# A fused chunk-selecting attention and gated feed-forward kernel: nine wide filler products as 36 narrow ones, and block 4's transposes ahead of two loads

## The chip, the cores and the metric

The kernel runs on one core of a Trainium2 chip. The metric is the device time of one execution in microseconds (us). A comparison takes the median of several runs. The profiled execution is one further run, whose instructions and transfers were all recorded; its times count from the first instruction.

## What is computed

Attention over 4 batches of 8 heads, 768 tokens and 64 elements a head, followed by a feed-forward layer. Each query picks, of the chunks of 32 keys up to its own, the six with the highest upper bound of the score, and attends to their keys alone:

```python
k_min, k_max = k_chunks.min(axis=3), k_chunks.max(axis=3)
ub = np.maximum(q * k_min, q * k_max).sum(-1)        # per query and chunk
ub = np.where(causal, ub, -1e9)
top_chunks = np.argsort(ub, axis=-1)[..., -6:]
scores = np.where(sel & (key <= query), scale * q @ k.T, -1e9)
x = softmax(scores) @ v                              # 3072 tokens x 512
xn = x / sqrt(mean(x * x) + 1e-6) * rms_g
g = xn @ w_gate                                      # 512 x 1536
out = (g * sigmoid(g) * (xn @ w_val)) @ w_out        # 1536 x 512
```

## The kernel before, in words

**Blocks.** The work is cut into twelve blocks of 256 queries of one batch, numbered in the order `ORDER` of line 340; block 4 is batch 0, queries 256 to 511, which the trace's steps call `(0, 1)`. A block goes through two stages. Attention (`job` and `pick`, lines 486 to 859): load q and k (`load_qk`, line 431), turn them on VectorE (line 636), reduce k's chunks (line 651), upper bounds on TensorE (lines 522 and 540), the choice on VectorE (lines 565 to 593), masked scores on TensorE (lines 760 and 771), exponentials on ScalarE (line 810), products with v (line 836), normalised x (line 855). Feed-forward (`norm` and `ffn`, lines 862 to 1032): x is scaled by its root mean square, transposed into `xsT`, multiplied with the gate and value weights (line 960), and the gated result with the output weights (line 1008).

**The order is written out by hand.** Each step of the program is an operation `plan.op` with a number. The list `STEPS` (line 47) says in which order the operations are issued, over all engines; each engine executes its own in that order. An entry x of zero or more is operation x // 8 on engine x % 8 (0 TensorE, 1 ScalarE, 2 VectorE, 3 GpSimd, 4 SyncE). `SLOTS` (line 156) gives, in the order of `STEPS`, the buffer that each operation takes. Semaphores follow from what each instruction reads and writes.

**Fillers.** A negative entry puts products between the steps of TensorE that nobody reads, into a PSUM buffer that is free at that place; they keep TensorE at work while it would wait. In `run`, line 236, the entry is decoded: `n, slot = divmod(-x, 16)`, then n // 2 products into buffer `slot`, wide if n is odd. Line 1075 issues them: the identity as weights, and as the moving side the identity once (narrow, 128 columns) or four times over (wide, 512 columns). Each product is two instructions of TensorE, a weight load and the product. Fillers wait for nothing but their PSUM buffer. Before the first upper bounds stand 75 narrow ones; 39 wide ones follow in the first 33 us.

**Block 4's way to `xsT`.** From block 4 on, the transposition of x is done by DMA (`norm`, lines 885 to 900). For each half of 128 tokens: `scale4s` on VectorE (line 890) multiplies x by its factor and the weights of the norm and writes a buffer `xs`; `across4s` on SyncE (line 896) issues a DMA that writes the transposed half into `xsT`. The gate products of block 4 (line 960) read both halves. SyncE also issues all loads of q and k (line 376, loads of 64 KB) and all stores (line 1030), one after the other; a step that waits holds up everything behind it on this queue. The steps of SyncE around the place are, in the order before: store of block 2's second half, two loads of q for block 8 (`load q1210`, `load q1220`: batch 1, third block, part, group), `across40`, `across41`, `load q1201`, then four copies of q between partitions (line 706).

Of the kernel before, what the change touches and what calls it, by code (L numbers as in the profile page):

```python
# [33 lines left out]
class Plan:  # L34
# [13 lines left out]
        131, 228, 233, 123, 155, 3, 99, 249, 244, 27, 257, 276, 83, 34, 203, 281, 67, 268, 107, 291,  # L48
        75, 115, 412, 425, 299, 433, 420, 538, 139, 466, 380, 396, 473, 482, 490, 404, 545, 42, 498,
        388, 522, 506, 515, 179, 594, 529, 611, 315, -2080, -320, 616, 562, 601, 672, 554, 626, 571,  # L50
        681, 50, 578, 457, 786, 587, 634, 323, -82, -82, 792, 642, 689, 57, 848, 650, 802, 699, 810,
        9, 818, 857, 307, 658, 865, 665, 826, 875, 834, 1098, -176, 704, 841, 443, -80, 736, 912,
        713, 746, 922, 754, 721, 1107, 930, 1185, 1042, -82, -114, 880, 451, 1114, 1049, 1058, 19,
        731, 889, 1066, 331, 897, 1130, 961, 1075, -338, -114, 1248, 1170, 760, 1257, 1082, 1091,
        907, 1660, 1177, 195, 971, -83, 936, 1628, -80, 1192, 1644, 1362, 977, 1138, 1684, 1265,
        1676, 1202, 1147, 1210, -112, 984, 1668, 770, 1154, 1163, 778, 1123, 1636, 946, -49, 1368,
        954, 1652, 1218, 1001, 1275, 994, 1424, 1433, 1226, -51, 1312, 1378, 8384, 1011, 1234, 1441,
        1322, 1242, 1386, 8344, 1330, 147, 1451, 1017, 1394, 1402, 339, 1280, 1410, 8369, 1418,
        1024, 1289, 1488, 347, 8336, 1498, 1297, 1034, 355, 8401, 1506, 1456, 8353, 8480, 1307,
        8410, 1537, 363, 8362, 1336, 8497, 8488, 1547, 1346, 1473, 1762, 8528, 1465, 8506, 1851,  # L60
# [30 lines left out]
        3323, 4940, 9377, 4980, 3339, 3256, 3353, 4972, 3842, 3280, 4900, 9584, 4459, 3290, 3361,  # L91
        4932, 3266, 3850, 9531, 9632, 3274, 9601, 3298, 3857, 3368, 9610, 5548, 3392, 3378, 9649,
        4956, 9627, 9640, 3386, 3402, 4964, 3417, 3410, 3864, 5580, 9658, 4275, 3425, 5644, 9680,
        5002, 3873, 9356, 4363, 5106, 4948, 3889, 3435, 5564, 5066, 9665, 9388, 3458, 3904, 4465,
        5628, 3442, 9675, 5612, 9712, 3913, 5018, 3883, 3452, 5026, 3899, 3921, 5090, 3468, 5042,
        3976, 5082, 4472, 5059, 3985, 5604, 5122, 5035, 4411, 4001, 9688, 4482, 3995, 9720, 9697,
        5139, 4016, 4490, 4498, 5049, 4011, 5148, 3928, 9729, 6308, 3952, 4025, 3938, 6356, 5098,
        9792, 3962, 4506, 5172, 4033, 9840, 3970, 5156, 3946, 9809, 4514, 5164, 4040, 9865, 9800,
        9818, 5620, 4521, 6332, 4050, 5714, 9832, 5572, 5114, 5588, 4592, 9849, 5179, 5652, 4058,
# [67 lines left out]
        0, 0, 1, 0, 2, 11, 3, 1, 0, 3, 0, 1, 1, 0, 2, 1, 1, 1, 1, 0, 1, 0, 0, 2, 3, 4, 1, 0, 6, 1,  # L167
        0, 0, 1, 0, 1, 2, 0, 1, 2, 2, 1, 0, 0, 2, 1, 0, 0, 0, 1, 3, 0, 1, 0, 1, 2, 0, 2, 3, 3, 0, 7,
        12, 2, 1, 0, 1, 0, 0, 0, 3, 0, 2, 3, 1, 0, 2, 8, 1, 2, 2, 3, 2, 0, 1, 2, 2, 1, 9, 3, 0, 1,
        0, 2, 0, 1, 0, 13, 0, 0, 0, 1, 0, 1, 10, 2, 1, 4, 0, 1, 1, 0, 1, 3, 1, 2, 0, 0, 1, 1, 0, 0,  # L170
        3, 1, 0, 0, 3, 3, 1, 0, 2, 0, 2, 4, 5, 0, 0, 3, 2, 1, 0, 0, 0, 0, 2, 1, 0, 2, 0, 0, 11, 3,
        14, 2, 1, 15, 1, 1, 2, 2, 0, 1, 1, 0, 0, 1, 3, 1, 2, 2, 0, 0, 3, 1, 2, 0, 0, 0, 1, 0, 2, 0,
        4, 1, 1, 2, 1, 0, 1, 3, 1, 2, 4, 1, 0, 0, 1, 2, 1, 0, 1, 1, 3, 1, 2, 1, 3, 0, 0, 16, 0, 2,
        2, 5, 0, 1, 0, 1, 0, 3, 0, 0, 1, 1, 1, 2, 0, 12, 0, 2, 1, 0, 1, 1, 3, 9, 0, 2, 1, 1, 2, 0,
        1, 5, 2, 3, 0, 0, 1, 1, 1, 0, 2, 1, 0, 6, 1, 3, 2, 2, 0, 2, 2, 1, 0, 0, 1, 0, 0, 1, 7, 8, 0,
        3, 2, 12, 9, 1, 0, 0, 1, 1, 1, 0, 2, 3, 0, 2, 1, 3, 0, 2, 1, 0, 0, 1, 0, 3, 2, 0, 2, 2, 0,
        3, 0, 2, 0, 0, 0, 1, 1, 0, 1, 2, 0, 0, 0, 3, 0, 4, 0, 13, 1, 1, 1, 0, 1, 0, 3, 2, 0, 1, 0,
        0, 2, 0, 2, 10, 0, 2, 3, 1, 1, 1, 1, 1, 1, 0, 0, 2, 2, 1, 0, 0, 0, 1, 1, 5, 1, 3, 1, 0, 2,
        0, 2, 0, 11, 1, 0, 0, 0, 0, 3, 2, 0, 3, 3, 3, 12, 1, 0, 1, 1, 1, 5, 0, 2, 4, 1, 0, 0, 2, 3,
        1, 0, 0, 0, 1, 0, 1, 2, 2, 2, 0, 3, 1, 1, 1, 0, 0, 2, 1, 0, 0, 2, 0, 3, 0, 0, 2, 0, 1, 1, 3,  # L180
        4, 1, 1, 0, 1, 2, 2, 2, 1, 1, 3, 0, 0, 0, 0, 1, 0, 2, 1, 2, 3, 0, 3, 2, 1, 2, 8, 0, 2, 3, 2,
        0, 6, 1, 0, 1, 2, 1, 8, 1, 9, 0, 0, 2, 3, 0, 0, 1, 1, 0, 0, 1, 0, 2, 1, 1, 0, 2, 0, 0, 0, 3,
        1, 2, 1, 0, 2, 2, 2, 0, 0, 1, 0, 7, 1, 3, 3, 1, 0, 2, 2, 2, 0, 0, 1, 1, 3, 1, 2, 9, 1, 0, 2,
        1, 0, 3, 0, 2, 2, 1, 3, 1, 1, 0, 5, 2, 0, 1, 1, 0, 3, 10, 2, 2, 0, 2, 1, 2, 3, 2, 1, 0, 0,
        11, 0, 3, 1, 3, 1, 0, 2, 0, 1, 1, 0, 0, 2, 12, 1, 1, 1, 0, 0, 0, 2, 1, 0, 2, 2, 2, 1, 2, 3,
        1, 0, 4, 6, 1, 0, 1, 3, 2, 1, 1, 0, 2, 5, 1, 1, 0, 0, 1, 0, 0, 2, 0, 1, 0, 3, 1, 2, 8, 0, 4,
        3, 1, 0, 1, 3, 2, 2, 2, 2, 0, 0, 1, 1, 3, 0, 2, 2, 0, 2, 3, 1, 9, 3, 0, 0, 2, 2, 0, 1, 2, 3,
        1, 5, 2, 0, 1, 1, 2, 0, 0, 2, 1, 0, 3, 2, 10, 0, 1, 11, 0, 1, 2, 2, 3, 1, 0, 0, 2, 0, 2, 7,
        3, 0, 2, 0, 2, 0, 3, 1, 0, 4, 3, 0, 6, 1, 0, 1, 3, 0, 12, 2, 0, 0, 1,
# [917 lines left out]
```

## Time and profile before

| | |
|---|---|
| time, median of 3 runs | 291.84 us (291.59 to 293.34) |
| the profiled execution's own time | 291.08 us |
| its span, first to last instruction | 289.3 us |
| its mean granted TensorE clock | 1.000 |
| ScalarE busy | 206.6 us (71%) |
| GpSimd busy | 168.4 us (58%) |
| VectorE busy | 216.3 us (75%) |
| data moved by DMA | 31.94 MB, mean 110 GB/s |

In the profile PE is TensorE's products, PEld its weight loads, DVE is VectorE, ACT ScalarE, POOL GpSimd, SP SyncE; an engine's name with a q is its instruction queue. A row of a timeline gives the start, the length, the engine, the line of the kernel, the operation, what it writes and reads, how many instructions were merged, and in brackets the idle time before and what ended it. A row of windows gives the stretch, its length, and for the engine the busy time and the number of instructions; then the granted clock, the DMA share and the rate. A row of a DMA queue gives packets, MB, and the share of 16 DMA engines that the packets took.

### The profile page before, as it was taken

The page shows a single profiled execution, that of the slowest core. Times are in us where ns is not written, and L with a number is a line of the kernel's source. Part 1 is how long each engine was busy: PE and PEld are TensorE (multiplying, and loading weights), DVE is VectorE, ACT ScalarE, POOL GpSimd, SP SyncE. Part 2 cuts the span into 40 slices and gives each one's busy share as a digit, 9 for nine tenths or more (in the row PEclk, how much of TensorE's full clock was granted, in tenths as well). Part 3 has the DMA queues.
Part 4 walks back from the last instruction along what each step waited for, and adds up shares of the span by engine and source line. Part 5 has one row for each costly group of instructions (what it writes and reads, how often), then busy time and mean ns, then how long its engine had stood idle before and what let it go on. Part 6 is the DMA issues. An engine that isn't in the chain of part 4 may idle for free.

```text
span 289.3 us, 11429 instructions
## 1 busy us (share of the span) xinstructions
PE 278.8 (96%) x4706; PEld 214.8 (74%) x4734; DVE 216.3 (75%) x626; ACT 206.6 (71%) x355; POOL 168.4 (58%) x268
## 2 busy tenths in 40 slices
PE   7998999999999997999999999999999999999995
PEld 7646997758877856888776786788678967588763
DVE  3889788798998998699989999987574724274332
ACT  2976787778988987867966695877679767564421
POOL 6797789979987874567693485527225206112420
PEclk9999999999999999999999999999999999999999
DMA  8999999988499495468699506902012200303013
GB/s 189 195 193 243 207 202 141 149 149 131 108 172 157 117 189 94 108 97 160 99 180 145 148 22 102 128 5 75 2 36 78 22 2 3 111 18 58 0 49 134
DMA packets 86388, 31.94 MB, mean 110 GB/s; under 512 B 74816, under 2 KB 81728, under 8 KB 86336
## 3 DMA queue, kind: packets, MB, share of 16 engines
q1 hardware_dynamic: 55616, 22.56, 34.0%
q0 software_dynamic: 29712, 7.87, 27.4%
q10 hardware_dynamic: 1008, 0.79, 1.3%
q8 instruction: 37, 0.61, 0.9%
q14 instruction: 15, 0.12, 0.1%
HBM read 28.58 MB, written 6.29 MB: 121 GB/s over the span
## 4 chain that ended last, share of the span: by engine, by line
PE 90%; DMA 4%; ACT 2%; SPq 1%; issue 1%; DVE 1%; ACTq 0%
PE F L960 45%; PE F L1008 19%; PE S L760 8%; PE F L836 7%; PE F L1075 3%; PE S L771 3%; PE F L522 3%; PE F L540 1%; DMA xsT<-xs 1%; SPq L376 1%; DMA kraw<-in_k_dram 1%; DMA qraw<-in_q_dram 1%; ACT kb L643 1%; PE F L916 1%; DVE kx L651 1%
## 5 line engine op out<-in xcount | busy, mean ns | idle before, releaser
L810 ACT ACTIVATE pt<-S 128x1024 bf16<-128x1024 f32 (+3 forms) x104 | 85.5, 858 | 29.8 <-PE S L771 25.9
L982 POOL TENSOR_TENSOR hh<-tg,vs 128x512 bf16<-128x512 bf16 x48 | 55.6, 1167 | 44.4 <-DVE tg L971 27.5
L960 PE MATMUL F<-xsT,wg 128*128 128x256 bf16 (+1 forms) x640 | 72.2, 262 | 1.5 <-DMA xsT<-xs 1.5
L960 PE MATMUL F<-xsT,wv 128*128 128x256 bf16 (+1 forms) x640 | 71.6, 262 | 0.1
L971 DVE SCALAR_TENSOR_TENSOR tg<-th,F 128x512 bf16<-128x512 bf16 x72 | 48.4, 679 | 25.9 <-ACT th L967 20.5
L1008 PE MATMUL F<-wo,hh 128*128 128x512 bf16 (+1 forms) x272 | 65.5, 370 | 1.8 <-issue 0.6
L960 PEld LDWEIGHTS <-wg 128*128 128x128 bf16 x640 | 56.0, 98 | 10.3 <-issue 2.0
L960 PEld LDWEIGHTS <-wv 128*128 128x128 bf16 x640 | 56.2, 98 | 7.8 <-issue 0.2
L967 ACT ACTIVATE th<-F 128x512 bf16<-128x512 f32 x72 | 42.6, 599 | 13.8 <-PE F L960 12.6
L780 POOL TENSOR_SCALAR_AFFINE_SELECT pt<-pt 128x512 bf16<-128x512 bf16 x48 | 31.9, 670 | 26.5 <-ACT pt L810 26.4
L1008 PEld LDWEIGHTS <-hh 128*128 128x128 bf16 x300 | 27.6, 98 | 25.2 <-issue 0.4
L979 ACT ACTIVATE vs<-F 128x512 bf16<-128x512 f32 x48 | 28.5, 599 | 9.6 <-PE F L960 6.4
L760 PE MATMUL S<-qb,kb 32*128 32x256 bf16 (+1 forms) x800 | 32.9, 253 | 1.2 <-issue 1.0
L651 DVE TENSOR_REDUCE kx<-kT 128x16 f32<-128x512 f32 x48 | 31.1, 670 | 0.2
L836 PEld LDWEIGHTS <-pt 128*128 128x128 bf16 x672 | 25.4, 98 | 3.8 <-issue 0.2
L836 PE MATMUL F<-VX,pt 128*128 128x65 bf16 x672 | 27.4, 194 | 0.2
L760 PEld LDWEIGHTS <-kb 32*128 32x128 bf16 x800 | 13.9, 92 | 14.2 <-issue 12.8
L975 DVE TENSOR_TENSOR hh<-tg,F 128x512 bf16<-128x512 bf16 x24 | 16.1, 682 | 10.4 <-PE F L960 10.1
L376 POOL DMA_DIRECT2D VX<-in_v_dram x24 | 22.8, 952 | 0.0
L771 PE MATMUL S<-mtd,chunkrow 32*128 32x128 bf16 (+2 forms) x384 | 20.4, 203 | 0.0
L855 DVE TENSOR_TENSOR xnat<-F,rden 128x256 bf16<-128x256 f32 x48 | 19.5, 415 | 0.7
L771 PE MATMUL S<-mto,chunkrow 32*128 32x128 bf16 (+2 forms) x384 | 19.9, 203 | 0.0
(73 smaller groups left out, 339.1 us busy)
## 6 DMA issues: line engine op xcount, KB each, us to landing
out_dram<-osb SPq DMA_DIRECT2D x23, 256.0 KB, 3.3
kraw<-in_k_dram SPq DMA_DIRECT2D x72, 64.0 KB, 3.2
qraw<-in_q_dram SPq DMA_DIRECT2D x72, 64.0 KB, 3.2
VX<-in_v_dram POOLq DMA_DIRECT2D x24, 128.0 KB, 4.9
QX<-qT SPq DMA_DIRECT2D x32, 64.0 KB, 2.8
wv<-in_moe_w_val_dram POOLq DMA_DIRECT2D x3, 512.0 KB, 9.7
wg<-in_moe_w_gate_dram POOLq DMA_DIRECT2D x3, 512.0 KB, 8.6
wo<-in_moe_w_out_dram POOLq DMA_DIRECT2D x3, 512.0 KB, 11.5
```

The lines of the kernel that those rows point to most:

```text
L651: plan.op(f"ext{n}{J}", "DVE", 0.585, 0.67, lambda n=n, op=op: VE.tensor_reduce(out=at(kx)[:, g, n], in_=at(kT).rearrange("p h (j c x) -> ...
L760: TE.matmul(s[a // 2][:, a % 2, c0:c0 + q1 - q0], kbt[r, t, ks], qbt[r, t, q0:q1], start=(t == 0), stop=(t == 1 and not mask), skip_group_ ...
L771: TE.matmul(o, chunkrow[r, BLK * kg + P * e:BLK * kg + P * (e + 1)], mv, start=False, stop=(d == 1), skip_group_check=True)
L780: GE.affine_select(out=d, in_=d, compare_op=ALU.is_ge, fill=0.0, base=0, pattern=[[0, 4], [1, P]], channel_multiplier=-1)
L810: lambda pt=pt, hs=hs, c0=c0, c1=c1, x=sc[hp]: SE.activation(out=at(pt)[:, hs, c0:c1], in_=at(x)[:, :, c0:c1], func=ACT.Exp, scale=SCALE), ...
L836: TE.matmul(o[:, a, :], p_[:, a, off:off + P], vt[:, e, 4 * g + a, :], start=(kb_ == 0 and a == 0), stop=(kb_ == nkb - 1 and a == 3), skip ...
L960: TE.matmul(at(p_)[:, n * W:(n + 1) * W], w[:, g, ht * P:(ht + 1) * P], at(xT)[:, g, x0:x0 + W], start=(g == 0), stop=(g == NP - 1), skip_ ...
L967: plan.op(f"tanh{U}.{hp}", "ACT", 0.48, 0.6, lambda th=th, gp=gp: SE.activation(out=at(th), in_=at(gp), func=ACT.Tanh, scale=0.5), pri - 0 ...
L971: VE.scalar_tensor_tensor(out=at(tg), in0=at(th), scalar=1.0, in1=at(gp), op0=ALU.add, op1=ALU.mult), pri - 30, reads=[th, gp], writes=[tg ...
L979: plan.op(f"vcopy{U}.{hp}", "ACT", 0.48, 0.6, lambda vs=vs, vp=vp: SE.activation(out=at(vs), in_=at(vp), func=ACT.Copy), pri + 0.1, reads= ...
L982: plan.op(f"hh{U}.{hp}", "POOL", 1.11, 1.16, lambda tg=tg, vs=vs, hh=hh: GE.tensor_tensor(out=at(hh), in0=at(tg), in1=at(vs), op=ALU.mult) ...
L1008: TE.matmul(at(op)[:, cs], at(key)[:, o:o + P], wo[:, ht, cs], start=(ht == 0), stop=(ht == NHT - 1), skip_group_check=True)
```

## The change

Two things are edited, both in the lists. First, three negative entries near the start of `STEPS`. Before, `-82, -82` stand for two and two wide products into buffer 2, ahead of the upper bounds of block 0's second group of heads; now `-514` stands for 16 narrow ones into the same buffer. Before, `-176` stands for five wide products into buffer 0, ahead of the first masked scores; now `-640` stands for 20 narrow ones. The columns that are computed stay the same, 9 x 512 = 36 x 128. TensorE has 27 more products and 27 more weight loads, so 54 more instructions, ahead of all that follows. Counted in blocks of 256 instructions of TensorE, each later limit falls on an instruction that came 54 earlier in the program before.

```diff
-        681, 50, 578, 457, 786, 587, 634, 323, -82, -82, 792, 642, 689, 57, 848, 650, 802, 699, 810,
-        9, 818, 857, 307, 658, 865, 665, 826, 875, 834, 1098, -176, 704, 841, 443, -80, 736, 912,
+        681, 50, 578, 457, 786, 587, 634, 323, -514, 792, 642, 689, 57, 848, 650, 802, 699, 810, 9,
+        818, 857, 307, 658, 865, 665, 826, 875, 834, 1098, -640, 704, 841, 443, -80, 736, 912, 713,
```

Second, the steps around block 4's transposes. 3458 and 3442 are `scale41` and `scale40` on VectorE, which change places; 3452 and 3468 are `across40` and `across41` on SyncE; 5628 and 5612 are `load q1210` and `load q1220`, which go behind them one by one (5604 is `load q1201`):

```diff
-        5002, 3873, 9356, 4363, 5106, 4948, 3889, 3435, 5564, 5066, 9665, 9388, 3458, 3904, 4465,
-        5628, 3442, 9675, 5612, 9712, 3913, 5018, 3883, 3452, 5026, 3899, 3921, 5090, 3468, 5042,
-        3976, 5082, 4472, 5059, 3985, 5604, 5122, 5035, 4411, 4001, 9688, 4482, 3995, 9720, 9697,
+        5002, 3873, 9356, 4363, 5106, 4948, 3889, 3435, 5564, 5066, 9665, 9388, 3442, 3904, 4465,
+        3458, 9675, 9712, 3452, 3913, 5018, 3883, 5026, 3899, 3921, 5628, 5090, 3468, 5042, 3976,
+        5082, 4472, 5059, 5612, 3985, 5122, 5035, 5604, 4411, 4001, 9688, 4482, 3995, 9720, 9697,
```

| | SyncE's order | VectorE's order |
|---|---|---|
| before | store 2.1, load q1210, load q1220, across40, across41, load q1201 | scale41, scale40 |
| after | store 2.1, across40, load q1210, across41, load q1220, load q1201 | scale40, scale41 |

The orders of TensorE, ScalarE and GpSimd stay as they were. `SLOTS` changes in five lines: the two halves of blocks 4, 6, 8 and 10 change their `xs` buffers with each other, and those of blocks 7 and 10 their buffers of x (`xnat`).

20 rows, old and new, of tables (SLOTS, STEPS) are left out of this document.

## The prediction

> **What bounds the kernel now.** I read the page first, then the waits of TensorE, then TensorE's timeline around its two longest waits, and last the DMA view and the other queues at those two places.
>
> ```profile
> span 289.3 us, 11429 instructions
> ...
> PE 278.8 (96%) x4706; PEld 214.8 (74%) x4734; DVE 216.3 (75%) x626; ACT 206.6 (71%) x355; POOL 168.4 (58%) x268
> ...
> q8 instruction: 37, 0.61, 0.9%
> ...
> PE 90%; DMA 4%; ACT 2%; SPq 1%; issue 1%; DVE 1%; ACTq 0%
> ```
>
> The first line is the span. The profiled execution took 291.08 us, so 1.8 us lie around the span; it is 0.8 us below the median of the three runs, 291.84. TensorE (PE) is busy for 96% of the span, and the chain that ended last lies on it for 90%. So a time that TensorE gains or loses is a time of the whole kernel, unless a later wait takes it up. The q8 line is a queue that carries nothing but instructions: 37 packets, 0.61 MB, 16.5 KB each. TensorE's recorded instructions, 4706 products (PE) and 4734 weight loads (PEld), divided by 37 give 255: one packet is one block of 256 instructions of TensorE.
>
> ```profile
> PE F L960 <- DMA xsT<-xs: 1.5, 1, 1.5
> PE S L760 <- issue: 1.0, 1, 1.0
> PE F L1008 <- issue: 0.6, 4, 0.2
> ```
>
> These rows give who waited for whom, the total in us, how often, and the longest. After its start TensorE stands still twice for over 1 us. The first wait is for the transposed x of a block (xsT), the second "for issue", which means that no semaphore explains it. The third row is four pieces of at most 0.2 us. So 2.5 us are all that could be won in the middle of the run, and both parts of the change point at one of these places.
>
> ```profile
> 27.69 0.10 PEld L760 LDWEIGHTS <-kb 32*128 32x128 bf16 x4
> 28.96 0.10 PEld L760 LDWEIGHTS <-kb 32*128 32x128 bf16 x4 [1.17 <-issue]
> ```
>
> In the timeline of the weight loads the second wait is seen from close by. It falls inside the scores of block 1: four loads at 27.69, and the next four of the same line only at 28.96, 1.17 us idle. Nothing that TensorE would wait for lies between two such groups, so I take it for a block of instructions that was not there yet. That can be tested with positions. The windows below count weight loads from the start (the number behind the x); each product has one load, so twice the count is the position in the program.
>
> ```profile
> 0.00:9.06 9.06, 6.78 (x93) 1.00 0.98 187
> 0.00:15.44 15.44, 10.23 (x221) 1.00 1.19 191
> 0.00:22.90 22.90, 14.23 (x349) 1.00 1.30 192
> 0.00:28.50 28.50, 18.56 (x477) 1.00 1.27 205
> 0.00:35.38 35.38, 24.84 (x606) 1.00 1.27 205
> ```
>
> The stall comes after load 477 (row to 28.50). One block earlier, 128 loads, is load 349, issued at 22.90; another 128 earlier, less one for two semaphore instructions between, is load 222, issued at 15.44; then load 94 at about 9.06; and one block behind the stall is 605 at 35.38. Now the packets of q8, in four windows of the DMA view of 0.2 us each: 12.6 to 12.8, 26.3 to 26.5, 32.8 to 33.0, 38.6 to 38.8. Each row is one packet that begins there; its share times 16 engines times 0.2 us is its length.
>
> ```profile
> q8 instruction: 1, 0.02, 37.8%
> q8 instruction: 1, 0.02, 36.1%
> q8 instruction: 1, 0.02, 32.1%
> q8 instruction: 1, 0.02, 27.9%
> ```
>
> The lengths are 1.21, 1.16, 1.03 and 0.89 us. So TensorE enters a block at 9.06 and a packet begins at 12.7; it enters one at 22.90 and a packet begins at 26.4, ends at 27.56, and TensorE goes on at 28.96, 1.4 us after the packet's end; it enters one at 28.96, and a packet begins at 32.9. I read this as: **on entering a block TensorE asks for the next one, and here it can use that block 6.06 us later** (22.90 to 28.96). A block that takes longer than that costs nothing, a shorter one stalls. From 9.06 to 15.44 it was 6.38 us, from 28.96 to 35.38 it was 6.42: both just long enough. The limits in this stage are all close to a stall, and 54 instructions decide it.
>
> **The change, part 1: nine wide products become 36 narrow ones.** The durations first.
>
> ```profile
> 9.84 1.04 PE L1075 MATMUL F<-ident 128*128 128x512 bf16 x4
> 10.91 0.44 PE L540 MATMUL F<-qT,BO 64*64 64x32 f32 x16
> 11.84 1.25 PE L1075 MATMUL F<-ident 128*128 128x512 bf16 x5
> 13.02 0.29 PE L760 MATMUL S<-qb,kb 32*128 32x128 bf16 x8
> ```
> ```profile
> 2.00:5.50 3.50, 3.43 (x34) 1.00 0.98 279
> 7.00:8.50 1.50, 1.48 (x27) 1.00 1.46 187
> ```
>
> Four wide products lie between 9.84 and the second upper bounds at 10.91, five between 11.84 and the scores at 13.02: 1.07 and 1.18 us, waits at their ends included. Of narrow ones, 34 loads fall into 3.5 us early on (103 ns each) and 27 into 1.5 us later (56 ns each). At 56 ns the new 16 take 0.90 us and the new 20 take 1.12 us, 0.2 us less than the wide ones; at the early rate they take 1.65 and 2.06 us, 1.5 us more. I take the later rate, which lies nearest in time, and count nothing, since what follows hides either: TensorE comes to a block that is not there for 1.9 us. If that cover is gone, -0.2 to +1.5 us counts.
>
> The cost is the place of the limits. 27 more products are 54 more instructions, all of them in by load 163 of today. So from there on a limit that stood at load n now stands where load n-27 stands today. The limit of load 222 moves to load 195, that of 349 to 322, of 477 to 450, of 605 to 578. When are these issued today?
>
> ```profile
> 0.00:13.36 13.36, 9.20 (x195) 1.00 1.17 191
> 0.00:22.14 22.14, 13.73 (x323) 1.00 1.29 192
> 0.00:27.04 27.04, 17.92 (x451) 1.00 1.28 206
> 0.00:33.87 33.87, 23.33 (x578) 1.00 1.27 205
> ```
>
> At 13.36, 22.14, 27.04 and 33.87. Now the sum, limit by limit.
> - Load 195, 13.36: the block is asked for at 9.06 as before, since nothing before 9.84 changes. Its packet ends at 12.7 + 1.2 = 13.9, and 1.4 us later, at 15.3, it can be used. **TensorE stands from 13.36 to 15.3, 1.9 us.** Bounds: 0.5 us if the packet's end at 13.9 were enough, 2.1 us from 15.44, when the block was in use without a wait. I take 1.9, by the one stall that shows both ends. Nothing later takes it up: the products up to 18.7 are fillers and scores in a fixed order, and the waits above show no further idle time of TensorE until 27.69 that isn't tied to its own results.
> - Load 322, 22.14 + 1.9 = 24.05: asked for at 15.3, there at 21.4. No stall.
> - Load 450, 27.04 + 1.9 = 28.9: asked for at 24.05, there at 30.1. It stalls 1.2 us, and today's stall of 1.26 us at load 477 goes: -0.1 us.
> - Load 578, 33.87 + 1.8 = 35.7: asked for at 30.1. From the packet row at 32.9 that takes 3.9 + 1.03 + 1.4 = 6.3 us, from the one at 38.7 (entered at 35.38) it takes 3.3 + 0.89 + 1.4 = 5.6 us. So a stall between 0 and 0.7 us; I take 0.4.
> - Later limits: no wait for issue above 0.2 us is in the rows after 35.38. I take nothing.
> Sum of part 1: +2.2 us, between +0.5 and +2.9.
>
> [...]
>
> **The change, part 2: block 4's transposes.** VectorE scales half 0 before half 1, and SyncE (SP) now issues: transpose 40, load, transpose 41, load, in place of two loads and then both transposes. The buffers of scaled x and of x change places with the order; each new holder is read by the same kind of instruction at the same place, so that costs nothing.
>
> ```profile
> 102.87 0.45 SPq L376 DMA_DIRECT2D qraw<-in_q_dram  x1
> 104.98 0.54 SPq L1030 DMA_DIRECT2D out_dram<-osb  x1
> 105.57 1.56 SPq L376 DMA_DIRECT2D qraw<-in_q_dram  x2
> 107.23 2.63 SPq L896 DMA_TRANSPOSE xsT<-xs  x2
> 109.91 1.55 SPq L376 DMA_DIRECT2D qraw<-in_q_dram  x1
> ```
> ```profile
> 103.55 2.27 DVE L890 SCALAR_TENSOR_TENSOR xs<-xnat,ri_all,gB 128x512 bf16<-128x512 bf16 x2
> ```
> ```profile
> 108.60 3.95 DMA xsT<-xs
> 112.69 1.91 PE F L960 x16
> ```
>
> Today the store ends at 105.52, the two loads take 1.56 us (a load at 102.87 takes 0.45, so one of them waited), and the two transposes are issued from 107.23 to 109.86. The second starts at 108.60 and lands 3.95 us later; TensorE starts at 112.69, having waited 1.50 us since 111.19. The two scalings run from 103.55 to 105.82, so the first is done before 105.52 unless it takes 2 of the 2.27 us, and transpose 40 can be issued right behind the store: 105.57 to 106.9. One load follows, 0.45 to 1.1 us, and transpose 41 starts between 107.3 and 108.0, which is 0.6 to 1.3 us earlier. Its packets also have one load of 64 KB less ahead of them on the queue. So it lands at 111.3 to 112.0. Against TensorE's arrival at 111.19 this alone would win 0.7 to 1.4 us. Both loads are passed: the first goes out 1.3 us later than today, the second some 3 us later, at about 109.
>
> ```profile
> qraw<-in_q_dram SPq DMA_DIRECT2D x72, 64.0 KB, 3.2
> ...
> 115.13 0.71 DVE L636 STREAM_TRANSPOSE qT<-qraw 128x512 f32<-128x512 f32 x1
> ```
>
> A load of q lands after 3.2 us by the median, so at 112.3, and VectorE first turns that block's q at 115.13: 2.8 us of cover, and if that were gone, 64 KB at 3.2 us would stand in VectorE's way.
>
> With part 1 TensorE arrives 2.2 us later, and the scaled x depends on TensorE's values just before. Is VectorE late by as much?
>
> ```profile
> 97.00:113.00 16.00, 15.53 (x52) 1.00 0.71 133
> 113.00:121.00 8.00, 5.13 (x16) 1.00 0.44 102
> ```
>
> It is busy for 15.53 of 16 us there, so it has next to no slack to catch up in, and I take it to be late by the same. Whatever it is less late by narrows the wait. I take -1.3 us, bounds -0.6 and -1.5. Afterwards VectorE is idle for 2.9 of 8 us, so it can follow a TensorE that no longer stops, and I see no next wait behind.
>
> **Sum:** +2.2 - 1.3 = +0.9 us. Against the profiled execution that is 292.0 us, against the median 292.7 us. One per cent is 2.9 us, about what a measurement of this kernel can tell from no change.
>
> **The rivals.**
> - *The limits cost nothing* (chance 0.2). If the block that is used at 15.44 was there well before 13.36, no stall comes, and the one at 28.96 goes: -1.3 - 1.4 = -2.7, 289.2 us. For it: most limits pass without a wait, and 15.44 only bounds that block from above. Against it: its packet begins at 12.7. [...]
> - *The transposes win nothing* (0.1). SP now stands at transpose 40 until half 0 is scaled. If VectorE is late by the whole 2.2 us and the transpose still takes 3.95 us to land behind the earlier loads, the wait at 111.19 stays. Then +2.2, 294.0 us. It decides from the point where transpose 41 lands 1.5 us behind TensorE's arrival. Against it: one load less stands ahead.
> - *TensorE's clock falls back* (0.05; slower). The early narrow loads take 103 ns, those from 7.0 us on 56 ns (the clock column says 1.00 in both), so TensorE runs at half pace from 2.07 to a time between 5.5 and 7.0, 3.4 to 4.9 us. A stop of 1.9 us at 13.36, so soon after, could bring that back for as long, which costs half of it, some 2.1 us: 294.8 us. It decides only if a stop of 1.9 us is enough; one of 1.26 us at 27.69 was not. [...]
> - *Only the stall at 13.36 stays away*, the later limits are as worked out (0.05): +0.9 us less 1.9, 290.8 us.
> - The forecast: 0.6, by its own bounds from 290.8 to 294.1, likely 292 to 293.5.
>
> **How the numbers follow.** The time is the forecast's, 292.7. The range from 289.1 to 294.5 leaves out half of the first rival and all of the clock's. Below 288.9 (faster by over 1%) lies only the edge of the first rival, 0.04; above 294.8 the clock and the forecast's worst ends, 0.07; the rest is within 1%.
>
> **What would show it.** Right: a stop of TensorE near load 222, around 13.4 to 15.3, inside the first masked scores; a second near load 477 at about 29 to 30, now inside a gate product of block 0; no wait for xsT near 112 to 114, and transpose 40 issued right behind the store. Wrong: no stop between 13 and 16 us, or a stop elsewhere than at loads 222, 477 and 605, which would mean that blocks are asked for otherwise; a wait of over 1 us for xsT; narrow products at 100 ns behind the stop.

## The result and the profile after

The changed kernel takes 295.38 us, the median of nine runs (293.16 to 297.64), against 291.94 us for nine runs of the kernel before beside it. The ratio is 1.0102, with a 95% interval from 1.0068 to 1.0137: slower by 3.4 us by the medians, where 0.9 us was forecast. The time lies outside the range of the prediction. The profiled execution took 295.75 us.

The page of the changed kernel: the span, the engines, the queue of instructions, the chain that ended last.

```profile
span 294.0 us, 11484 instructions
...
PE 280.2 (95%) x4733; PEld 216.2 (74%) x4761; DVE 216.4 (74%) x626; ACT 206.6 (70%) x355; POOL 168.0 (57%) x268
...
q8 instruction: 37, 0.61, 0.9%
...
PE 78%; DMA 7%; DVE 5%; issue 4%; ACT 2%; SPq 2%; ACTq 0%; DVEq 0%
```

There are 55 more instructions, and TensorE's busy time grew by 1.4 us of a span that grew by 4.7. So most of what came is standing still. The chain says where to look: "issue" had 1% and has 4%, DMA had 4% and has 7%.

What TensorE waited for in the changed kernel (total, times, longest):

```profile
PE S L771 <- issue: 1.5, 1, 1.5
PE F L960 <- DMA xsT<-xs: 1.4, 1, 1.4
PE F L960 <- issue: 1.3, 2, 0.9
PE F L540 <- DVE BO L676: 0.7, 1, 0.7
PE F L1008 <- issue: 0.6, 4, 0.2
PE F L836 <- DVE hh L975: 0.4, 1, 0.4
PE F L540 <- issue: 0.3, 1, 0.3
PE F L960 <- DVE tg L971: 0.3, 1, 0.3
```

Four waits for issue of over 0.2 us stand in place of one (the four of line 1008 were there before), the wait for xsT is still there, and two short ones for VectorE are new. Now TensorE's timeline at its start, weight loads left aside:

```profile
10.72 1.07 PE L1075 MATMUL F<-ident 128*128 128x128 bf16 x16
...
12.70 1.29 PE L1075 MATMUL F<-ident 128*128 128x128 bf16 x20
13.92 0.29 PE L760 MATMUL S<-qb,kb 32*128 32x128 bf16 x8
...
15.88 0.18 PE L771 MATMUL S<-mto,chunkrow 32*128 32x32 bf16 x1 [1.47 <-issue]
```
```profile
30.02 0.56 PE L960 MATMUL F<-xsT,wg 128*128 128x128 bf16 x7 [0.45 <-issue]
...
36.77 0.62 PE L960 MATMUL F<-xsT,wv 128*128 128x128 bf16 x8 [0.90 <-issue]
...
43.35 0.24 PE L540 MATMUL F<-qraw,BO 64*64 64x32 f32 x2 [0.34 <-issue]
```
And the same places counted in weight loads:
```profile
0.00:15.80 15.80, 10.63 (x222) 1.00 1.14 177
0.00:29.60 29.60, 19.24 (x477) 1.00 1.25 195
0.00:36.00 36.00, 24.66 (x605) 1.00 1.23 195
0.00:43.00 43.00, 30.61 (x732) 1.00 1.23 196
```

The stops come at loads 222, 477, 605 and 732. They are 255, 128 and 127 loads apart; at two instructions a load that is one or two blocks of 256 instructions. The 16 and 20 narrow products took 1.07 us and 1.22 us (12.70 to 13.92), where the wide ones took 1.07 and 1.18 us.

To see where the 4.7 us came from, I matched each weight load of the changed kernel with its counterpart before (27 places earlier) and took the difference of their starts. It is +0.84 us ahead of everything that was changed (a wait for the first bounds, `BO`, which lies between 0.2 and 1.6 us in the profiles of this study), +2.51 behind load 222 (16 us), +1.74 behind load 477, +2.83 behind 605, +3.35 behind 732, +3.57 at 97 us, +3.52 at 130, +4.42 at 174 and +4.74 at the end. So part 1 cost 1.67 - 0.77 + 1.09 + 0.52 = 2.5 us, part 2 won nothing at block 4, and another 1.2 us came behind it. The 0.84 us at the start are no part of the change.

SyncE's queue and VectorE around block 4's transposes: one row of SyncE from before, then SyncE and VectorE of the changed kernel:

```profile
101.39 0.94 SPq L376 DMA_DIRECT2D qraw<-in_q_dram  x2
```
```profile
104.75 2.31 SPq L376 DMA_DIRECT2D qraw<-in_q_dram  x2
...
109.84 0.39 SPq L1030 DMA_DIRECT2D out_dram<-osb  x1
110.33 1.35 SPq L896 DMA_TRANSPOSE xsT<-xs  x1
111.74 0.56 SPq L376 DMA_DIRECT2D qraw<-in_q_dram  x1
112.40 2.38 SPq L896 DMA_TRANSPOSE xsT<-xs  x1
```
```profile
107.11 2.27 DVE L890 SCALAR_TENSOR_TENSOR xs<-xnat,ri_all,gB 128x512 bf16<-128x512 bf16 x2
```

Between these two profiles the stretch from the store to the second transpose shrank from 3.62 us (104.98 to 108.60) to 2.56 us, by 1.06 us. VectorE's scaling is 3.56 us later than before, TensorE comes to the gate products 3.58 us later (114.77 instead of 111.19). But the store ahead of the transposes was issued 4.86 us later. **SyncE lost 1.3 us more than TensorE, and that took the 1.06 us back**: the wait for xsT is 1.44 instead of 1.50 us. The first rows of SyncE's two fences show where: the same two loads took 0.94 us before and 2.31 us now, and the store and the transposes stand behind them.

Two things in the other profiles of this study qualify this. First, the order is not worth 1.06 us by itself. e1_narrow keeps the old order (the experiments follow below), and its SyncE shows:

```profile
110.43 0.40 SPq L1030 DMA_DIRECT2D out_dram<-osb  x1
110.87 0.96 SPq L376 DMA_DIRECT2D qraw<-in_q_dram  x2
111.93 2.64 SPq L896 DMA_TRANSPOSE xsT<-xs  x2
```

From the store to the second transpose (113.31) that is 2.88 us, and in e3_later, also with the old order, 2.90 us. Where none of the passed loads is slow, the new order wins some 0.3 us; in the profile of before they took 1.56 us instead of 0.96. Second, which load is slow differs from one execution to the next: in e0_after, the changed kernel once more, it was a load of k (1.65 instead of 0.45 us). What stays is the distance between the two engines. In the profiles with the new order the gate products wait where TensorE comes 4.9 to 5.5 us after the store was issued (1.44, 0.91 and 0.80 us in after, e0_after and e5_later_order), and by 0.1 us or not at all where it comes 6.5 to 7.6 us after it (e6_cover, e7_ahead, e2_order).

### The profile page after: what moved, and what is told of

It is laid out like the page before. It is cut to its first block, busy times and chain, and to the rows that moved or that the text cites. A ratio compares the mean times of both kernels' runs of the same rounds, so it can differ in the third digit from the quotient of the medians.

```text
span 294.0 us, 11484 instructions
## 1 busy us (share of the span) xinstructions
PE 280.2 (95%) x4733; PEld 216.2 (74%) x4761; DVE 216.4 (74%) x626; ACT 206.6 (70%) x355; POOL 168.0 (57%) x268
## 3 DMA queue, kind: packets, MB, share of 16 engines
q10 hardware_dynamic: 1008, 0.79, 1.3%
## 4 chain that ended last, share of the span: by engine, by line
PE 78%; DMA 7%; DVE 5%; issue 4%; ACT 2%; SPq 2%; ACTq 0%; DVEq 0%
PE F L960 39%; PE F L1008 17%; PE S L760 6%; PE F L836 6%; PE F L1075 3%; PE S L771 2%; SPq L376 2%; DMA qraw<-in_q_dram 2%; DMA xsT<-xs 2%; PE F L522 2%; PE F L540 2%; DMA out_dram<-osb 1%; DMA kraw<-in_k_dram 1%; ACT pt L810 1%; DVE tg L971 1%
## 5 line engine op out<-in xcount | busy, mean ns | idle before, releaser
L771 PEld LDWEIGHTS <-chunkrow 32*128 32x128 bf16 x768 | 18.6, 93 | 2.5 <-issue 1.6
L1023 ACT ACTIVATE osb<-F 128x512 f32<-128x512 f32 (+1 forms) x18 | 10.3, 574 | 14.3 <-PE F L1008 8.9
```

What stands on the lines that cost most here:

```text
L771: TE.matmul(o, chunkrow[r, BLK * kg + P * e:BLK * kg + P * (e + 1)], mv, start=False, stop=(d == 1), skip_group_check=True)
```

## The experiments

All are timed against the kernel before on the same chip (291.9 to 292.0 us there). Only `STEPS` and, where buffers change places with it, `SLOTS` are edited.

**Each part alone.** e1_narrow is part 1 with the steps of block 4 as before; e2_order is part 2 with the nine wide fillers.

```diff
 e1_narrow:  -82, -82 -> -514     -176 -> -640
 e2_order:   across40, load q1210, across41, load q1220 (as in the change)
```

> Part 1 alone: 36 narrow products for the nine wide ones, the steps around block 4's transposes as before. Theory (limits: a block of TensorE's instructions can be used some 6 us after it is asked for): the same stops as in the changed kernel, at loads 222 (1.5 to 2 us), 477 (0.4 to 1.2), 605 (0.9) and 733 (0.3 to 0.5), so +2.5 us by 45 us into the run. If part 2 wins its 1 us in the changed kernel, this one takes about 296.4 us; if part 2 wins nothing there, about 295.4. Rival (part 1 costs nothing, part 2 costs all): 290.6 to 292 us.

> Part 2 alone: transposes ahead of the two loads, nine wide products as before. Theory (the transposes are issued 1 us earlier behind the same store, and TensorE is not late): the wait for xsT falls from 1.5 us to 0.1 to 0.8, 290.5 to 291.2 us. Rival (the loads that are passed, or the queue's own lateness, take it back): the wait stays, 291.9 us, or some other wait opens and it is slower.

e1_narrow took 295.21 us, 1.0104 [1.0047, 1.0160]; e2_order 291.10 us, 0.9964 [0.9933, 0.9996]. So part 1 alone is as slow as the whole change, and part 2 alone is worth some 0.9 us. The two longest waits of TensorE in e2_order, after its start:

```profile
PE S L760 <- issue: 1.5, 1, 1.5
PE F L836 <- issue: 0.9, 1, 0.9
```

No wait for xsT is left there (1.50 us before). But the stops at loads 222 and 477, whose limits are where they were, put this execution back by 0.9 us against the profile of before, so they vary by about half a microsecond from run to run (0.4 and 1.5 us here, none and 1.0 in before); and a wait for issue of 0.9 us at 97.86 is new, at load 1622. So TensorE came to the gate products at 112.88 instead of 111.19, and that alone would have ended the wait; it is the time of twelve runs, not this profile, that shows a gain. Part 1 alone shows something else. Its TensorE in two stretches of 3.41 us:

```profile
12.29:15.70 3.41, 1.64 (x52) 1.00 1.25 212
15.70:19.11 3.41, 3.41 (x16) 0.50 1.33 204
```

Behind the stop (1.77 us at 13.87) the granted clock was 0.50 for 3.41 us, which by an estimate, half of the 3.41 us, put the products behind it back by some 1.7 us more than the stop itself. The changed kernel's profile at the same place has no such stretch, but in six of its nine runs the mean clock was 0.994 or less, which is what 3.4 us at half clock make of 294. This asks for a repetition (below).

**Is it the place of the limits?** e3_later makes 36 narrow products from nine wide ones too, but the nine stand behind the later scores of block 0, beyond load 222. e4_four changes only the first four wide ones, so the limits move by 24 instructions and not by 54.

```diff
 e3_later:   -338, -114 -> -1154, -146   (-82, -82 and -176 stay)
 e4_four:    -82, -82 -> -514            (-176 stays)
```

> Nine other wide products become 36 narrow ones: nine of the thirteen behind the second masked scores, loads 244 to 252, behind the limit of load 222. The same 54 instructions more, but the limit of load 222 stays where it was. Theory (limits): no stop at load 222; stops at 477 of 1.2 to 1.4 us, at 605 of 0.8 and at 733 of 0.3 us; +0.8 to +1.1 us in all, 292.7 to 293.0 us. Rival (narrow products are dear in themselves, wherever they stand): as part 1 alone, +2.5 to +3.5 us.

> Only the first four wide products become 16 narrow ones, 24 instructions more. The limit of load 222 then stands at what was load 210, inside the five wide fillers that end at 15.4 us. Theory (limits): a stop of about 0.3 us at load 222, 1.3 at 477, 0.5 at 605; +0.8 us, 292.7 us. Rival (a price per narrow product): 16 of 36 of what part 1 alone costs, +1.1 to +1.5 us, with no stop at a limit.

e3_later took 291.91 us, 0.9998 [0.9965, 1.0031]; e4_four 293.12 us, 1.0024 [0.9989, 1.0059]. The same number of narrow products costs nothing where they leave load 222 alone, and the stop there is 0.85 us with 24 instructions and 1.5 to 2.0 us with 54. So neither the narrow form nor the number is the cost; the place of the limits is. The sizes of both were missed. e3_later came out faster than expected (+0.8 to +1.1 us), since its stop at 477 is 0.6 us long and not 1.2 to 1.4, and there is none at 605 or 732. e4_four stops longer than expected: 0.85 us at 222 (0.3), 1.73 at 477 (1.3), none at 605 and 0.77 at 732; its interval includes 1, so its time alone doesn't decide. e3_later's longest waits:

```profile
PE F L960 <- DMA xsT<-xs: 0.7, 1, 0.7
PE F L1008 <- issue: 0.6, 4, 0.2
PE F L960 <- issue: 0.6, 1, 0.6
```

**The change again, and a cover for its stop.** e0_after is the changed kernel once more. e6_cover puts ten wide fillers, 2.2 us of products, behind the 20 narrow ones: TensorE should then come to load 222 as late as its block does (15.88 us in the changed kernel's profile).

```diff
 e6_cover:   -640 -> -640, -336
```

> The changed kernel once more, beside the three others on one chip. 295.4 us or 1.0% over the kernel before, as measured; the stops at loads 222, 477, 605 and 733 again, each within 0.5 us of what the first profile shows, since they hang on transfers that don't land at the same time in each run.

> The changed kernel with ten more wide fillers (2.2 us of TensorE) right behind the 20 narrow ones, just ahead of the scores in which it stops at load 222. Theory: the stop is set by the block's arrival at 15.3 to 15.9 us, so the ten run in it and cost nothing: the stop at 222 falls below 0.6 us, and the time is not above the changed kernel's by more than 0.4 us. And if it is the stop that brings the half clock (granted clock of 0.992 to 0.994 in six of nine runs of the changed kernel), runs with such a clock become rare and the median falls to some 294.4 us. Rival for the clock (it comes whatever TensorE does there): as many such runs, 295.4 us or more. Rival for the stop (TensorE's own work is the bound there): 2.2 us slower, 297.5 us.

e0_after took 296.08 us, 1.0097 [1.0054, 1.0141]; e6_cover 295.01 us, 1.0092 [1.0058, 1.0127]. Of e0_after's stops at the four loads only those at 222 (1.85 us) and 605 (0.35) are over 0.3 us. Ten products of 0.22 us more cost nothing by the times, as if they filled a hole that was there anyway (1.85 us in e0_after). The stop at load 222 is gone from e6_cover's profile, but in that execution the clock was at half from 11.77 to 15.19 us, which by the same estimate alone makes TensorE 1.7 us later there, so the profile doesn't show that the ten products were enough. The median did not fall to 294.4 us. In e0_after's profile the clock fell as in e1_narrow's, behind a stop of 1.85 us:

```profile
12.06:15.47 3.41, 1.55 (x51) 1.00 1.26 199
15.47:18.88 3.41, 3.41 (x16) 0.50 1.29 206
```

while the changed kernel's first profile had a stop of 1.47 us and kept its clock:

```profile
13.79:17.20 3.41, 1.94 (x49) 1.00 1.31 200
17.20:20.61 3.41, 3.41 (x47) 1.00 1.29 207
```

Of the runs of e0_after 4 in 12 had a mean clock of 0.994, with a median of 297.1 us against 295.0 for the others; of e6_cover's, 1 in 12. In the profiles of e0_after and e1_narrow the clock falls right behind the stop, in some executions only; in e0_after that goes with 2 us. That the stop at load 222 is what makes such runs frequent is not shown: the kernel before, whose profile has no stop there, had a mean clock of 0.994 or less in 4 of 29, 10 of 35 and 5 of 17 runs beside these experiments, and e0_after's runs without the fall are still 3.5 us above those of the kernel before (295.0 against 291.4 on the same chip).

**Does part 2 win behind limits that don't stop TensorE?** e5_later_order is e3_later with part 2. e7_ahead is the changed kernel with three loads (q1230, k1230, k1210) moved from ahead of block 4's transposes to behind them.

```diff
 e7_ahead (SyncE):  ..., load k1230, load q1230, ..., load k1210, store2.1, across40, load q1210, across41, ...
                 -> ..., store2.1, across40, load q1210, across41, load k1230, load q1230, load k1210, ...
```

> Part 2 together with the other 36 narrow products, those behind the limit of load 222 (loads 244 to 252), the first nine wide as before. Theory: both gains hold, no stop at 222, a stop of 0.6 us at 477 in place of 1.3, no wait for xsT; 290.5 to 291.1 us, at least as fast as part 2 alone (291.1). Rival (part 2 wins only where TensorE is not shifted at all): 291.9 us.

> The changed kernel with three more loads of block 8 (k1230, q1230, k1210) put behind the second transpose of block 4, so that the transposes are issued some 1.5 us earlier on SyncE. Theory (in the changed kernel SyncE comes to the transposes late, with the halves long scaled): the wait for xsT falls from 1.3 us to below 0.4, 294.2 to 294.6 us or 0.3% less than the changed kernel beside it. Rival (the scaling on VectorE or the transfer itself sets the landing): the wait stays over 1 us and the time too.

Both missed. e5_later_order took 292.49 us, 0.9995 [0.9958, 1.0031], no better than e3_later without part 2, and its profile waits 0.80 us for xsT where e3_later's waits 0.70. e7_ahead took 295.42 us, 1.0110 [1.0074, 1.0145], no better than the change, although its wait for xsT is gone. What was won at block 4 (by TensorE's lateness against before, 3.14 us ahead of it and 1.48 behind) is given back some 16 us later. Of e7_ahead (its lines count one more than the others'), TensorE, then VectorE, then GpSimd:

```profile
129.74 1.03 PE L961 MATMUL F<-xsT,wg 128*128 128x256 bf16 x8 [0.57 <-DVE tg L972]
131.52 0.80 PE L837 MATMUL F<-VX,pt 128*128 128x65 bf16 x20 [0.75 <-DVE tg L972]
132.72 0.92 PE L837 MATMUL F<-VX,pt 128*128 128x65 bf16 x24 [0.40 <-DVE hh L976]
```
```profile
125.40 2.15 DVE L891 SCALAR_TENSOR_TENSOR xs<-xnat,ri_all,gB 128x512 bf16<-128x512 bf16 x2 [0.76 <-POOL ri_all L881]
```
```profile
121.50 1.20 POOL L734 TENSOR_SCALAR qraw<-QX 128x512 f32<-128x512 f32 x2 [6.98 <-DMA QX<-qT]
```

Read from the bottom: GpSimd waits 6.98 us for SyncE's copies of q (line 706), so the scale factor of block 5 is late, so VectorE waits 0.76 us for it and scales late, and TensorE waits 1.7 us in three pieces for gated results. The same two steps in e2_order, where nothing is given back:

```profile
118.08 1.20 POOL L733 TENSOR_SCALAR qraw<-QX 128x512 f32<-128x512 f32 x2 [4.91 <-DMA QX<-qT]
```
```profile
122.61 1.79 DVE L890 SCALAR_TENSOR_TENSOR xs<-xnat,ri_all,gB 128x512 bf16<-128x512 bf16 x2
```

GpSimd waits 2 us less, and VectorE does not wait. The three waits of TensorE, 1.7 us in sum, stand alike in e0_after and e5_later_order. They are missing in e6_cover, the changed kernel with the cover, where the wait for xsT is 0.1 us and nothing is given back by 150 us.

**Are SyncE's copies the next bound?** In e8_copies, e9_later_copies and e10_order_copies the four copies go ahead of five loads, on top of the changed kernel, e5_later_order and e2_order. Two of the five (k1230, k1210) stood ahead of block 4's transposes until then, and so did q1230, which now follows them; so the transposes go out earlier too.

```diff
 (SyncE):  ..., across41, load q1230, load q1220, qm0, qm3, qm1, qm2, load k1230, load k1210, load q1201, load q3100, load q3130, ...
```

> The changed kernel; on SyncE's queue load q1230 goes behind across41, and five more loads (k1230, k1210, q1201, q3100, q3130) go behind the four copies qm0, qm3, qm1, qm2(2,1). All other queues are in the order of the changed kernel. Theory (SyncE's queue is the next bound: its copies are late, so GpSimd's relu, its rms of block 5 and VectorE's scaling are late): the last copy ends at most 4 us behind TensorE's arrival at block 4's gate products, VectorE's scale of block 5 no longer waits for GpSimd, TensorE waits neither for xsT nor at 129 to 133 us; 293.4 to 294.0 us against 295.4 of the changed kernel, since 1.4 us of wait for xsT and 0.4 at 132 go. Rival (VectorE itself has no room left, whoever feeds it): waits of 1 us and more in sum stay at 129 to 133 us, and the time is 295 or more, as with the transposes ahead of three loads (295.4).

> The kernel with the nine narrow fillers behind the later scores and both transposes ahead (292.5), with the same loads behind SyncE's copies. Theory: the waits of 0.69 for xsT and of 0.57, 0.75 and 0.39 at 127.9 to 131.1 go: 290.1 to 291.0. Rival (VectorE has no room): the waits at 128 to 131 stay, 291.8 to 292.5.

> Part 2 alone (291.1) with the same loads behind SyncE's copies. There no wait for xsT and none at 129 to 133 us is left, so by both theories next to nothing is to be won: 290.8 to 291.3. If loads passed by the copies come too late themselves, slower than 291.4 with a new wait of VectorE for one of them.

All three have higher medians than what they were made from, though e8_copies's interval overlaps e0_after's: 298.43 us, 1.0180 [1.0128, 1.0233]; 295.69 us, 1.0104 [1.0076, 1.0132]; 295.43 us, 1.0059 [1.0015, 1.0104]. The theory held at its own place: in e8_copies the copies end at 117.5 instead of 119.1 us in e0_after, and VectorE scales block 5 without a wait. Then block 5's own transposes are late. SyncE and TensorE of e8_copies:

```profile
111.71 1.07 SPq L376 DMA_DIRECT2D qraw<-in_q_dram  x2
114.95 2.53 SPq L706 DMA_DIRECT2D QX<-qT  x4
...
128.93 1.23 SPq L896 DMA_TRANSPOSE xsT<-xs  x1
```
```profile
136.00 1.86 PE L960 MATMUL F<-xsT,wg 128*128 128x256 bf16 x8 [2.84 <-DMA xsT<-xs]
```

The copies stood at the head of the queue before their data were there: SyncE idled from 112.8 to 114.95, 2.2 us in which loads would have gone out. The transposes of block 5 were then issued at 128.93, 2.2 us after VectorE had scaled both halves (126.72), and TensorE stood for 2.84 us (2.44 and 2.73 us at the same place in the other two). And there the clock fell once more, at 135 us:

```profile
131.68:135.09 3.41, 1.48 (x56) 1.00 1.75 87
135.09:138.50 3.41, 2.50 (x12) 0.50 0.77 184
```

So neither theory that I had put up is right as it was put. SyncE's queue has no slack between 96 and 129 us in the profiles of before, after, e0_after, e5_later_order and e7_ahead: it shows no gap above 0.12 us there, and the last four are those with new waits of TensorE at 128 to 133 us. In e1_narrow, e2_order, e3_later, e4_four and e6_cover, which have no such waits, it idles for 0.3 to 2.8 us. In e8_copies to e10_order_copies it idles (2.2, 2.1 and 1.0 us ahead of the copies) because steps stand at its head before their data are there. So where the queue is full, what is pulled ahead on it makes something else late, be it the copies or block 5's transposes; that the full queue is the cause is read from these profiles, no experiment changed it alone.

## Why the prediction was wrong, point by point

- **That TensorE bounds the kernel** and that lost time there is lost for good was right: 2.51 us lost by 43 us were still lost at 97 us.
- **Narrow for wide at no cost** was right, to 0.04 us.
- **The bounds of part 1** are added up wrongly: its terms give +0.4 to +2.7 us, not +0.5 to +2.9; that changes nothing here.
- **"On entering a block TensorE asks for the next one."** Right in its places, though the asking itself is in no row of a profile: the stops came at the named loads (222, 477, 605), and e3_later and e4_four moved the limits and the stops with them. The sizes: the stop at 222 put TensorE back by 1.67 us (1.9 forecast), at 477 the stall shrank by 0.77 (0.1), at 605 it cost 1.09 (0.4), at 732 0.52 (none). The sum is +2.5 against +2.2; by its time part 1 alone cost 3.0 us by the ratio (1.4 to 4.7). The constant 6.06 us was the crude part: in the changed kernel the time from entering a block to using the next was 5.9, 5.4, 6.7 and 6.6 us, because the packet began 2.6 to 4.3 us after that entry; only the last stretch, 1.3 to 1.6 us from the packet's end, stayed the same. After 45 us, where some 31 limits lie (3960 loads in before), the profiles of before and of the changed kernel show no wait for issue above 0.2 us (four in each, at line 1008), so these limits cost next to nothing there; the four named ones stopped TensorE for 0.3 to 1.5 us, and so did in other runs the one at load 1622, where e2_order, e4_four and e10_order_copies stop for 0.6 to 0.9 us.
- **"I take it to be late by the same"** (VectorE) was right: 3.56 us against TensorE's 3.58.
- **"I take -1.3 us"** for part 2 is the step that failed. The reasoning asked only VectorE whether it was late, and took "transpose 40 can be issued right behind the store" for enough. It was issued right behind the store; but nobody had asked when the store is issued. SyncE's queue, full before already, had fallen 1.3 us behind TensorE, by two loads that took 1.37 us longer, and the wait for xsT stayed at 1.44 us, the prediction's own sign of being wrong (over 1 us). The term was also sized from one execution in which a passed load happened to be slow: two such loads take 0.96 us in e1_narrow, not 1.56, and then the order is worth some 0.3 us. By the times, part 2 won 0.9 us alone and nothing on top of part 1 (1.0102 and 1.0097 of the kernel before with it, 1.0104 without).
- **"I see no next wait behind"** failed as well. In the changed kernel two new waits of 0.4 and 0.3 us follow; in e0_after, e5_later_order and e7_ahead there are three that make 1.7 us. VectorE's idle 2.9 of 8 us was the wrong place to look: before, these are waits for TensorE (2.1 us) and ScalarE (0.6), while the wait that came is later, for block 5's scale factor from GpSimd, which waits for SyncE's copies.
- **The rivals.** "The transposes win nothing" (0.1, 294.0 us) is what happened, though not by its mechanism, VectorE. "TensorE's clock falls back" (0.05) happened in part of the executions on top, and in e0_after at about its price: 2.1 us, where its runs show 297.1 against 295.0. In e1_narrow the two such runs are no slower than the other four. I gave it 0.05, and the one stop that spoke against it, 1.26 us, was too short to tell: behind stops of 1.77 us (e1_narrow) and 1.85 us (e0_after) the clock was at half for 3.41 us, behind one of 1.47 us (the changed kernel) it was not. It is not needed for the miss: e0_after's runs at full clock have a median of 295.0 us, beyond 294.5, where the range ended.

What stays open: why those two loads took 1.37 us longer, and why in each execution another issue is slow; nothing was tested on it. It is open too why e5_later_order, 0.6 us later than e2_order at block 4's gate products (113.48 against 112.88), gave back 2.1 us behind them and e2_order nothing. Of the whole 3.4 us, 2.5 are the limits by the trace; the rest is the waits behind block 4 and the clock in part of the runs, and both change from run to run.

## What to carry to other kernels

Count instructions as well as microseconds: where a program runs close to the rate at which its instructions arrive (at the changed kernel's four stops a block could be used 5.4 to 6.7 us after the one before it was entered), 54 more of them ahead of a block's limit cost 2.5 us here though the engine's work is the same, and the same edit a little later cost nothing (e3_later, 0.9998). Before moving a step ahead on a queue, look at when the whole queue gets there and not only at what the step waits for; on a full in-order queue a gain at one place can be taken from the next (e7_ahead: no wait for xsT, then three waits of 1.7 us in sum). The only part that paid was the reorder alone (291.10 us), and not on top of either set of narrow products.

## What the hardware showed that was not expected

**The clock changed at whole multiples of 3.413 us.** In all thirteen profiles every change of the clock lies a whole multiple of 3.413 us from the others of its run, wherever the run began: full clock is on record for 283.31 us in before (83 of them, from 6.77 us on) and for 286.72 us in the changed kernel (84, from 6.96 us on), half clock for 3.41 us in e0_after, e1_narrow and e6_cover and, from 135.09 us on, for 6.83 us in e8_copies. The rows of windows above show what it goes with: stretches of this length in which products filled 1.64, 1.55 and 1.48 of 3.41 us (43 to 48%) were followed by one at half clock, 1.94 (57%) was not. Over the thirteen profiles there are six stretches below 49% between the start and 285 us, and five were followed by half clock; of fifteen between 50 and 70% one was (e6_cover, 67%). So the share of busy time does not decide alone. The one of the six that was not is in e10_order_copies:

```profile
131.42:134.83 3.41, 1.61 (x15) 1.00 0.51 145
134.83:138.24 3.41, 3.41 (x57) 1.00 1.18 160
```

So a stop of 1.77 us that fell wholly into one stretch was followed by half clock (e1_narrow), and one of 2.73 us that a border cut was not (e10_order_copies, 130.49 to 133.22). That would explain why the same kernel is longer in some executions; it was not tested.

**Ten more fillers ahead of the stop cost nothing.** Ten fillers of 0.22 us behind the 20 narrow ones took nothing from the time (295.01 against 296.08 us, the intervals overlap; 295.1 against 295.0 among the runs at full clock). In 11 of their 12 runs the clock stayed up; against 8 of 12 in e0_after that is too few to show that the cover did it.
